# A gated linear-attention and Mish MLP kernel: the SBUF pool moved up by 128 bytes, and the queries' denominators kept in an existing tile

## The chip, the cores and the metric

The kernel runs on one core of a Trainium2 chip, in one launch. The metric is the device time of one execution in microseconds (us), given as the median of several runs. The profile is one further execution, recorded instruction by instruction.

Engines are named as in the profile: PE (TensorE matmuls), PEld (TensorE's weight loads), DVE (VectorE), ACT (ScalarE), POOL (GpSimd), SP (SyncE, which issues most DMAs). A matmul has a *moving* operand, which is streamed through the array (512 columns here), and *weights*, the stationary operand, which a separate weight load puts into the array beforehand. Both lie in SBUF.

## The reference

x is 2048 x 512. Attention has 32 heads of width 16; the MLP is 1376 wide.

```python
g = sigmoid((x * gate_w).sum(-1, keepdims=True))
return g * A(x) + (1 - g) * B(x)

# A: linear attention with a learned feature map
q, k, v = split_heads(x @ wqkv)
pq, pk  = q @ w_phi[h], k @ w_phi[h]                      # 16 x 16 for each head
phi_q   = concat([softmax(pq), softmax(-pq)], -1)         # 32 features
phi_k   = concat([softmax(pk), softmax(-pk)], -1)
kv, z   = sum_s(phi_k^T v), sum_s(phi_k)
o       = (phi_q @ kv) / (phi_q @ z + 1e-6)
A       = o @ wo

# B: MLP
B = mish(x @ w1 + b1) @ w2
```

## The kernel before

**Split precision.** Every large product is made of three matmuls in fp32r: an operand is split into a high part ("h") and a low part ("l"), and h\*h, h\*l and l\*h are added up in PSUM. So all tiles that feed 512-column matmuls come in pairs: `xh`/`xl`, `wvh`/`wvl`, `w1ah`/`w1al`, `w2ah`/`w2al`, and so on. The high part is written by ACT (a copy), the low part by DVE or POOL (a subtraction).

**Stages.** First (P0) the key and query weights are multiplied by the feature map (`fuse`). Then eight chunks A0 to A7 of 256 rows go through the projections (`proj`), the features of the keys (max, min, exp, sum on DVE and ACT, in tiles `E`), and the sums `kvp` and `z`. Chunks 2 to 7 use a Strassen-like scheme: sums of the weights and of the rows stand in spare parts of the MLP's weight buffers, so that `proj` matmuls there have operands named `w1bhr`, `w1blr`, `w2bh`, `w2bl`. Then four blocks B0 to B3 of 512 rows do, for the MLP, `up` (moving: `xbh`/`xbl`; weights: slices of `w1a`/`w1b`) and `down` (moving: `w2a`/`w2b`; weights: slices of `h`/`l`), and for attention the queries' features, `num` and `wo` (moving: `woh`/`wol`; weights: slices of `ohl`). `up` has 12 matmuls of 512 columns for each of 11 units and block, in turn four of `xbh` with high weights, four of `xbh` with low weights, four of `xbl` with high weights.

**Order.** The order of all steps is written out by hand in `ORDER`, and each instruction is pinned to it (`pin`), so each engine runs its instructions in the order of that text. An engine that waits for another holds up all that stands behind it in its own order.

**The queries' denominators.** For each 128 rows of a block, on DVE: `dsum` reduces the products `T` to a tile `D` of 64 columns (two halves of 32 heads, tag `Dn`, two buffers); `dm` multiplies it by the swapped sums `S`; `de` adds the two halves into a tile `den` of 32 columns of its own (one buffer); `rd` takes its reciprocal in place; `sc` multiplies the swapped `S` by it and writes the factors into `D`; `es` (DVE or POOL) scales `E` by `D`; `tr` transposes `E` on DVE and `st` stores it by DMA.

**Where the tiles lie.** SBUF addresses below are bytes within a partition, as the compiled program of the kernel before has them. Tiles are put one behind the other: some constants, the "arena" of 45056 bytes (`nc.alloc_sbuf_tensor("arena", ...)`, into which the four `w1` tiles are placed by hand, line 121 on), the pool `const` (`onr`, `cst`, `ident`, `mask`, `kvb`), and the pool `sp` with all other tiles, in the order in which their tags first occur. All slices that 512-column matmuls take start at multiples of 512 bytes within their tile, so that a tile's own address decides the remainder modulo 256.

| tiles | address | modulo 256 |
|---|---|---|
| `w1bh`, `w1bl`, `w1ah`, `w1al` (arena) | 16512, 26752, 36992, 49280 | 128 |
| `onr` | 61568 | 128 |
| `cst` (128 bytes) | 62080 | 128 |
| `ident`, `mask`, `kvb` | 62208, 62720, 63232 | 0 |
| `io` and `v`; `xbh`/`wkh`, `xbl`/`wkl` | 65280 on; 71424, 79616 | 0 |
| `wvh`/`woh`, `wvl`/`wol`; `wqh` and `wql` (later `eT`) | 87808, 96000; 104192, 112384 | 0 |
| `w2ah`, `w2al`, `w2bh`, `w2bl`, `wc` | 120576 to 165632 | 0 |
| `act`, `h`, `l`, `xh`, `xl` (8 buffers) | 167680 to 194560 | 0 |
| `E` (4 buffers) | 180096; 196864, 209152, 215808 | 128; 0, 0, 0 |
| `ohl`, `xraw`, `T`, `pq`, `zb`, `Dn` and the rest | to 229120 | 0, but 128 for `mn` |
| `den` (128 bytes, the last tile) | 229120 | 0 |

So in `down` and `wo` and in most of `proj`, both operands lie at 0 modulo 256. In `up` the moving operand lies at 0 and the weights at 128. In some pairs of `proj` matmuls of chunks 2 to 7, one operand lies in the arena, at 128, and the other at 0.

Of the kernel before, what the change touches and what calls it, by code (L numbers as in the profile page):

```python
# [9 lines left out]
F32 = mybir.dt.float32  # L10
# [5 lines left out]
P = 128  # L16
S = 2048
D = 512
H = 32
# [70 lines left out]
def tile_gated_mix(ctx: ExitStack, tc: tile.TileContext, xT, wv, wkT, wqT, bd, w1a, w1b, b1, w2a, w2b, wo, out):  # L90
    nc = tc.nc
    const = ctx.enter_context(tc.tile_pool(name="const", bufs=1))
# [5 lines left out]
    V, G_, A_, Sy = nc.vector, nc.gpsimd, nc.scalar, nc.sync  # L98
# [4 lines left out]
    def pin(x):  # L103
        r = tc.keep_in_program_order(x)
        if hold[0] and dve and r.ins.engine == G_.engine:
            hold[0] = False
            tc.add_manual_dep(r.ins, dve[0].ins.name, SYNC, reason="VectorE's step first")
        return r
# [5 lines left out]
    def on_(e):  # L114
        return vv if e is V else pin
# [14 lines left out]
    def T(shape, dt, tag, bufs, name):  # L130
        if tag in FIXED:
            return FIXED[tag][dt]
        nm[0] += 1
        if bufs > 1 and slots:
            tag, bufs = tag + slots.pop(0), 1
        return sp.tile(shape, dt, name=f"{name}_{nm[0]}", tag=tag, bufs=bufs)

    def k8(name, tag, dt=F32R):
        return T([P, 2048], dt, tag, 1, name)

    def k4(name, tag, dt=F32):
        return T([P, 1024], dt, tag, {"E": 4, "tx": 2, "oh": 2, "z": 1}[tag], name)

    def k2(name, tag, dt=F32):
        return T([P, 512], dt, tag, {"pq": 2, "io": 4, "hl": 8}[tag], name)
# [14 lines left out]
    def hv(ap):  # L160
        return ap.rearrange("p (h f) -> p h f", f=DH)
# [32 lines left out]
    pin(G_.memset(md, 1.0))  # L194
    pin(G_.affine_select(md, md, pattern=[[-DH, 8], [0, DH]], compare_op=ALU.is_ge, fill=0.0, base=0, channel_multiplier=1))
    pin(G_.affine_select(md, md, pattern=[[DH, 8], [0, DH]], compare_op=ALU.is_ge, fill=0.0, base=DH - 1, channel_multiplier=-1))
    cst = const.tile([P, 32], F32, name="cst")
    b1s, g_sb, og_sb = cst[:, :NF], cst[:, 12:20], cst[:, 20:28]
    pin(G_.dma_start(b1s, b1))
    ident = const.tile([P, P], F32, name="ident")  # L200
# [9 lines left out]
    def at(key, name, fn):  # L210
        steps.setdefault((key, name), []).append(fn)
# [81 lines left out]
    def feat_ops(key, t, src, d, negative=False):  # L293

        n = str(t)

        def red(name, op):
            d[name] = T([P, H], F32, name, 2, name)
            pin(V.tensor_reduce(d[name], hv(src()), axis=AX.X, op=op))  # L299

        def dd(a, e=V):
            if "E" not in d:
                d["E"] = k4("E", "E")
            E = hv(d["E"][:, a * 512 : (a + 1) * 512])
            note = on_(e) if key[0] == "B" else pin
            if (a == 0) != negative:
                note(e.tensor_sub(E, hv(src()), d["mx"][:, :, None].to_broadcast([P, H, DH])))  # L307
            else:
                note(e.tensor_sub(E, d["mn"][:, :, None].to_broadcast([P, H, DH]), hv(src())))

        def ss():
            d["S"] = T([P, 2 * H], F32, "Sm", 2, "Sm")
            pin(V.tensor_reduce(d["S"], hv(d["E"][:, :]), axis=AX.X, op=ALU.add))  # L313

        at(key, "mx" + n, lambda: red("mx", ALU.max))
        at(key, "mn" + n, lambda: red("mn", ALU.min))
        for a in range(2):
            if key[0] == "B":
                for x, e in ENG:
                    at(key, f"d{a}{n}{x}", lambda a=a, e=e: dd(a, e))  # L320
            else:
                at(key, f"d{a}{n}", lambda a=a: dd(a))
        at(key, "E" + n, lambda: act(d["E"], d["E"], AF.Exp))
        at(key, "S" + n, ss)
        if key[0] == "A":
            at(key, "rS" + n, lambda: pin(V.reciprocal(d["S"], d["S"])))

    def scale_by(d, eng, by="S"):
        on_(eng)(eng.tensor_mul(hv(d["E"][:, :]), hv(d["E"][:, :]), d[by][:, :, None].to_broadcast([P, 2 * H, DH])))  # L329
# [346 lines left out]
    def b_ops(b):  # L676
        key = ("B", b)
# [88 lines left out]
        for t in range(4):  # L766
            d = {}
            i = 4 * b + t

            def lq(d=d, i=i):  # L770
                d["p"] = k2("pq", "pq")
                pin(Sy.dma_start(d["p"], pqd[i * P : (i + 1) * P, :]))

            def tm(e, d=d):
                d["T"] = k4("T", "tx")
                on_(e)(e.tensor_mul(d["T"], d["E"], B["zb"]))  # L776

            def dsum(d=d):
                d["D"] = T([P, 2 * H], F32, "Dn", 2, "Dn")
                pin(V.tensor_reduce(d["D"], hv(d["T"][:, :]), axis=AX.X, op=ALU.add))  # L780

            def halves(t):
                return t[:, :].rearrange("p (a h) -> p a h", a=2)

            def dm(d=d):
                pin(V.tensor_mul(halves(d["D"]), halves(d["D"]), halves(d["S"])[:, ::-1, :]))

            def de(d=d):
                d["d"] = T([P, H], F32, "den", 1, "den")
                pin(V.tensor_add(d["d"], d["D"][:, :H], d["D"][:, H:]))  # L790

            def sc(d=d):
                pin(V.tensor_mul(halves(d["D"]), halves(d["S"])[:, ::-1, :], d["d"][:, None, :].to_broadcast([P, 2, H])))

            def st(d=d, i=i):
                eTd[i] = tc.dram_tile([P, 1024], F32, name=f"eTd{i}")
                pin(Sy.dma_start(eTd[i][:, :], d["E"]))

            def ld(t=t, i=i):
                h = t // 2  # L800
                if h not in eTs:
                    eTs[h] = k8("eT", ("tt", "eT")[h], F32)[:, :].rearrange("p (t q x) -> p t q x", t=2, q=4)
                src = eTd[i].rearrange("(q i) (k x) -> k i q x", q=4, k=4)
                for k in range(4):
                    o = 64 * (k % 2) + 32 * (k // 2)
                    pin(Sy.dma_start(eTs[h][o : o + 32, t % 2, :, :], src[k]))

            at(key, f"lq{t}", lq)
            feat_ops(key, t, lambda d=d: d["p"][:, :], d)
            for x, e in ENG:  # L810
                at(key, f"T{t}{x}", lambda tm=tm, e=e: tm(e))
                at(key, f"es{t}{x}", lambda d=d, e=e: scale_by(d, e, "D"))
            at(key, f"D{t}", dsum)
            at(key, f"m{t}", dm)
            at(key, f"de{t}", de)
            at(key, f"rd{t}", lambda d=d: pin(V.reciprocal(d["d"], d["d"])))
            at(key, f"sc{t}", sc)
            at(key, f"tr{t}", lambda d=d: pin(V.transpose(d["E"][:, :], d["E"][:, :])))  # L818
            at(key, f"st{t}", st)
            at(key, f"ld{t}", ld)  # L820
# [60 lines left out]
    for b in range(NB):  # L881
        b_ops(b)
# [98 lines left out]
```

## Time and profile before

| | |
|---|---|
| median of 3 runs | 449.42 us (449.0 to 449.97) |
| the profiled execution | 449.53 us, of which the span from first to last instruction is 447.8 us |
| PE, PEld, DVE, ACT, POOL busy | 98%, 79%, 73%, 51%, 42% of the span |
| chain that ended last | PE 83%, DVE 13%, DMA 1%, issue 1% |
| its largest lines | `proj` 26%, `up` 22%, `down` 21%, `wo` 10% |
| TensorE clock granted | 0.996 of full speed |

A row of the profile's groups reads: line, engine, operation, output<-inputs, shapes, xcount, busy time in us, mean ns of one, idle time of that engine just before. For a matmul the moving operand is named ahead of the weights. The ends of matmuls are modelled, and neighbouring matmuls overlap, so that the busy time of one (some 390 ns) is not what it costs; the distance between starts is. The chain of waits gives such distances: it lists pieces as start in us, length in us, engine, tile, line and xcount, each piece reaching up to the start of the next one.

### The profile page before, as it was taken

To read this page: it belongs to the slowest core of one execution; us is meant where nothing else is said; L and a number is where in the kernel's file an instruction comes from. 1 tells how busy PE (TensorE), PEld (TensorE's weight loads), DVE (VectorE), ACT (ScalarE), POOL (GpSimd) and SP (SyncE) were. 2 spreads that over 40 slices of the span, in tenths; PEclk is the share of its full clock that TensorE was granted. 3 is DMA by queue.
4 is the path that set the end of the run, shared out by engine and by line. 5 is a ranking of instruction groups with operands and counts; after the bars stand their busy time and mean duration, and the time that the engine had idled before them with its cause. 6 is when DMAs were issued, how large, how long until landed. Compare 5 with 4: busy or idle time off the path is not lost.

```text
span 447.8 us, 7210 instructions
## 1 busy us (share of the span) xinstructions
PE 439.2 (98%) x2832; PEld 352.9 (79%) x2832; DVE 326.5 (73%) x433; ACT 227.7 (51%) x312; POOL 187.7 (42%) x139
## 2 busy tenths in 40 slices
PE   6999999999999999999999999999999999999996
PEld 5878888888788888877788878788887887888774
DVE  1699989998899799999896789337576673856212
ACT  4727626456465594863457375375452464243411
POOL 2466545668676166772325427330223021043110
PEclk8999999999999999999999999999999999999999
DMA  7422191988561342645133425002514301045202
GB/s 275 173 94 95 70 254 55 241 207 197 163 217 48 121 141 71 224 152 165 50 116 117 143 71 183 29 25 98 179 55 157 126 0 72 0 178 191 78 1 94
DMA packets 29033, 55.14 MB, mean 123 GB/s; under 512 B 5252, under 2 KB 13444, under 8 KB 29000
## 3 DMA queue, kind: packets, MB, share of 16 engines
q1 hardware_dynamic: 26952, 48.26, 31.7%
q0 software_dynamic: 1904, 6.17, 6.9%
q8 instruction: 22, 0.36, 0.3%
q10 hardware_dynamic: 144, 0.26, 0.2%
q14 instruction: 11, 0.09, 0.1%
HBM read 32.26 MB, written 22.03 MB: 121 GB/s over the span
## 4 chain that ended last, share of the span: by engine, by line
PE 83%; DVE 13%; DMA 1%; issue 1%; SPq 0%; ACT 0%; DVEq 0%
PE proj L128 26%; PE up L128 22%; PE down L128 21%; PE wo L128 10%; PE kvp L128 2%; DVE E L329 2%; PE num L128 2%; DMA w1ahf<-in_wkT_dram 1%; DVE Sm L313 1%; DVE Dn L780 1%; DVE den L790 1%; PE fuse L128 1%; DVE E L818 1%; DVE T L776 1%; DVE mn L299 1%
## 5 line engine op out<-in xcount | busy, mean ns | idle before, releaser
L701 POOL TENSOR_TENSOR l<-act,h 128x512 fp32r<-128x512 f32 x27 | 36.7, 1360 | 98.8 <-ACT h L155 89.4
L155 ACT ACTIVATE act<-up,cst 128x512 f32<-128x512 f32 x44 | 30.0, 686 | 56.4 <-PE up L128 44.9
L155 ACT ACTIVATE E<-E 128x1024 f32<-128x1024 f32 x32 | 33.5, 1057 | 19.3 <-DVE E L307 10.1
L128 PE MATMUL wo<-woh,ohl 128*128 128x512 f32 x128 | 42.0, 392 | 0.1
L155 ACT ACT_TABLE_LOAD x31 | 39.8, 1283 | 1.5 <-PE up L128 1.0
L155 ACT ACTIVATE h<-act 128x512 fp32r<-128x512 f32 (+1 forms) x48 | 30.1, 629 | 20.5 <-PE down L128 9.6
L313 DVE TENSOR_REDUCE Sm<-E 128x64 f32<-128x1024 f32 x32 | 38.5, 1205 | 2.4 <-ACT E L155 2.4
L128 PE MATMUL down<-w2ah,h 128*128 128x512 f32 x96 | 37.7, 392 | 0.0
L128 PE MATMUL down<-w2al,h 128*128 128x512 f32 x96 | 37.4, 390 | 0.0
L128 PE MATMUL down<-w2bh,h 128*128 128x512 f32 x80 | 31.9, 399 | 0.0
L128 PE MATMUL down<-w2ah,l 128*128 128x512 f32 x80 | 31.3, 391 | 0.0
L128 PE MATMUL down<-w2bh,l 128*128 128x512 f32 x80 | 31.3, 391 | 0.0
L128 PE MATMUL down<-w2bl,h 128*128 128x512 f32 x80 | 31.2, 390 | 0.0
L701 DVE TENSOR_TENSOR l<-act,h 128x512 fp32r<-128x512 f32 x13 | 11.9, 912 | 25.3 <-PE down L128 10.2
L128 PEld LDWEIGHTS wo<-woh,ohl 128*128 128x128 f32 x128 | 24.0, 188 | 5.8 <-DVE ohl L842 0.4
L867 DVE SCALAR_TENSOR_TENSOR io<-down,cst,io 128x512 f32<-128x512 f32 x16 | 11.6, 738 | 22.5 <-PE down L128 12.7
L818 DVE STREAM_TRANSPOSE E<-E 128x1024 f32<-128x1024 f32 x16 | 19.9, 1243 | 9.5 <-POOL E L329 9.1
L128 PE MATMUL up<-xbh,w1ahr 128*128 128x512 f32 x96 | 26.5, 397 | 0.0
L128 PE MATMUL up<-xbh,w1alr 128*128 128x512 f32 x96 | 26.2, 395 | 0.0
L776 POOL TENSOR_TENSOR T<-E,zb 128x1024 f32<-128x1024 f32 x7 | 18.1, 2582 | 19.5 <-ACT E L155 19.5
L128 PE MATMUL up<-xbl,w1ahr 128*128 128x512 f32 x96 | 26.2, 394 | 0.0
L842 DVE TENSOR_TENSOR ohl<-num,ohl 128x512 fp32r<-128x512 f32 x16 | 10.5, 686 | 21.3 <-ACT ohl L155 21.2
(195 smaller groups left out, 1102.6 us busy)
## 6 DMA issues: line engine op xcount, KB each, us to landing
eTd<-E SPq DMA_DIRECT2D x16, 512.0 KB, 3.0
eT<-eTd SPq DMA_DIRECT2D x64, 128.0 KB, 3.0
xraw<-in_xT_dram SPq DMA_DIRECT2D x15, 512.0 KB, 4.6
zd<-E POOLq DMA_DIRECT2D x10, 512.0 KB, 7.3
pqd<-qs SPq DMA_DIRECT2D x16, 256.0 KB, 2.6
pq<-pqd SPq DMA_DIRECT2D x16, 256.0 KB, 2.8
out_dram<-io SPq DMA_DIRECT2D x16, 256.0 KB, 2.1
raw<-in_w2a_dram SPq DMA_DIRECT2D x3, 512.0 KB, 5.1
```

Source lines behind the costliest of these rows:

```text
L128: return pin(nc.tensor.matmul(*a, **k))
L155: return pin(A_.activation(out_, in_, fn, **k))
L299: pin(V.tensor_reduce(d[name], hv(src()), axis=AX.X, op=op))
L313: pin(V.tensor_reduce(d["S"], hv(d["E"][:, :]), axis=AX.X, op=ALU.add))
L329: on_(eng)(eng.tensor_mul(hv(d["E"][:, :]), hv(d["E"][:, :]), d[by][:, :, None].to_broadcast([P, 2 * H, DH])))
L701: on_(e)(e.tensor_sub(U[i]["l"], U[i]["a"], f32(U[i]["h"])))
L776: on_(e)(e.tensor_mul(d["T"], d["E"], B["zb"]))
L780: pin(V.tensor_reduce(d["D"], hv(d["T"][:, :]), axis=AX.X, op=ALU.add))
L790: pin(V.tensor_add(d["d"], d["D"][:, :H], d["D"][:, H:]))
L818: at(key, f"tr{t}", lambda d=d: pin(V.transpose(d["E"][:, :], d["E"][:, :])))
L842: pin(V.tensor_sub(ohl[h, gp][:, 512:], num[h, gp], f32(ohl[h, gp][:, :512])))
L867: pin(V.scalar_tensor_tensor(io[t], dn[t], og_sb[:, i % 8 : i % 8 + 1], io[t], op0=ALU.mult, op1=ALU.add))
```

## The change

The tile `cst` grows from 32 to 64 columns (128 to 256 bytes for each partition); its parts stay where they are, and the added columns are used by nothing. The tile `den` is gone: the sum of the halves is written over the first half of `D`, its reciprocal is taken there, and `sc` now reads `S` in its own order and writes the halves of `D` in swapped order, the second half first, so that the denominators are overwritten last.

```diff
-    cst = const.tile([P, 32], F32, name="cst")
+    cst = const.tile([P, 64], F32, name="cst")
     b1s, g_sb, og_sb = cst[:, :NF], cst[:, 12:20], cst[:, 20:28]
...
+            def den(d):
+                return d["D"][:, :H]
+
             def de(d=d):
-                d["d"] = T([P, H], F32, "den", 1, "den")
-                pin(V.tensor_add(d["d"], d["D"][:, :H], d["D"][:, H:]))
+                pin(V.tensor_add(den(d), den(d), d["D"][:, H:]))
 
             def sc(d=d):
-                pin(V.tensor_mul(halves(d["D"]), halves(d["S"])[:, ::-1, :], d["d"][:, None, :].to_broadcast([P, 2, H])))
+                pin(V.tensor_mul(halves(d["D"])[:, ::-1, :], halves(d["S"]), den(d)[:, None, :].to_broadcast([P, 2, H])))
...
-            at(key, f"rd{t}", lambda d=d: pin(V.reciprocal(d["d"], d["d"])))
+            at(key, f"rd{t}", lambda d=d: pin(V.reciprocal(den(d), den(d))))
```

No instruction is added or taken away, and `ORDER` stays as it is.

## The prediction

> **What bounds the kernel now.** First the page's own lines: the profiled execution took 449.53 us with a span of 447.8, so 1.7 us lie around the span; the sum below is made against 449.53, which is 0.11 above the median of the runs (449.42).
>
> ```profile
> span 447.8 us, 7210 instructions
> PE 439.2 (98%) x2832; PEld 352.9 (79%) x2832; DVE 326.5 (73%) x433; ACT 227.7 (51%) x312; POOL 187.7 (42%) x139
> ```
>
> PE is never long without work, but its busy time is made of modelled ends. So I read next the chain of waits, in which a piece of matmuls reaches up to the next piece: length by count is the distance between starts. From it, in order of time:
>
> ```profile
> 139.94 2.80 PE up L128 x12
> ...
> 146.84 2.80 PE up L128 x12
> 149.64 1.97 PE kvp L128 x128
> 151.63 0.04 DVE km L645
> ...
> 204.44 1.18 DVE wol L617
> 205.62 0.61 DVE ohl L842
> 206.23 0.04 issue
> 206.28 5.32 PE wo L128 x22
> ...
> 222.37 16.75 PE up L128 x72
> ```
>
> ```profile
> 327.98 12.27 PE down L128 x54
> ...
> 391.23 8.37 PE up L128 x36
> 399.60 6.81 PE down L128 x30
> ...
> 418.09 2.73 PE wo L128 x12
> ...
> 443.74 0.75 DVE io L867
> ```
>
> Two things are to be seen. From 30 us to 151.6 and from 206.28 to 443.7 the chain is PE alone; between 151.63 and 206.2 it is DVE, whose steps follow each other without a wait for PE, until `wo` needs `wol` and `ohl`. PE is full there too, but it ends that stretch waiting, 0.4 us by the list of PE's waits:
>
> ```profile
> PE wo L128 <- DVE wol L617: 0.4, 1, 0.4
> ```
>
> And the same 128x512 matmul does not cost the same everywhere. `up`: 16.75/72 = 232.6 ns and 8.37/36 = 232.5, from start to start. `down`: 12.27/54 = 227.2 and 6.81/30 = 227.0. `wo`: 2.73/12 = 227.5. All three are of one shape and type and run at one clock. What sets `up` apart in the table of addresses is that its moving operand starts at 0 modulo 256 bytes and its weights at 128; in `down` and `wo` both start at 0. The difference is 5.2 to 5.4 ns; I take 5.2, since a row of `down` just behind `up` is a little slower than 227.
>
> Chunks 2 to 7 say more, since there operands in the arena mix with others from one pair of matmuls to the next. The timeline of PE in chunk 3 (start, modelled length, moving operand ahead of the weights):
>
> ```profile
> 93.71 0.62 PE L128 MATMUL proj<-wkh,xh 128*128 128x512 f32 x2
> ...
> 95.07 0.62 PE L128 MATMUL proj<-w2bh 128*128 128x512 f32 x2
> 95.53 0.62 PE L128 MATMUL proj<-w1blr,w2bh 128*128 128x512 f32 x2
> 95.98 0.63 PE L128 MATMUL proj<-w2bh,w1bhr 128*128 128x512 f32 x2
> 96.45 0.62 PE L128 MATMUL proj<-w2bl,w2bh 128*128 128x512 f32 x2
> ...
> 97.83 1.07 PE L128 MATMUL proj<-wvh,xh 128*128 128x512 f32 x4
> ```
>
> Six matmuls with all operands at 0 (93.71 to 95.07) take 1.36 us, 226.7 ns each; the six from 95.07 to 96.45, with one pair of mixed operands either way, take 1.38, and so do the next six.
>
> **The change part by part.**
>
> *The layout.* `cst` grows by 128 bytes, so all that is allocated behind it lies 128 bytes higher: `xbh`, `w2a`, `w2b`, `h`, `l`, `ohl`, `woh` and the other tiles of the pool go from 0 to 128 modulo 256. The arena and `onr` lie ahead of `cst` and stay at 128. Both operands of every 512-column matmul are then at 128: no mixed pair is left, and no pair is at 0 and 0. The trace of before has no long run with both at 128, so its price is bounded. Lower end: the pair that is alike at 0, 227.2 ns (nothing in the rows excludes one a little faster, but none shows it). Upper end: 232.6 ns, the price of weights at 128, if it is the weights' own remainder that costs. I take the lower end, because of the chunk's rows. If weights at 128 cost 5 ns by themselves, that had to show where they are loaded beside a moving operand that is at 128 too, which happens once in each such term: the load for `w2bh,w1bhr` runs beside the last matmul of the pair `w1blr,w2bh`. That pair took 95.98 - 95.53 = 0.45 us, 225 ns each, no more than an all-0 pair; the pair after it, moving at 0 and weights at 128, took 0.47, 235 each. The evidence is thin (one load for each term), and it speaks for the relation of the two operands.
>
> How many matmuls are concerned comes from the groups, first and last of the six of `up` (three of 96, three of 80: 528) and of the six of `down` (two of 96, four of 80: 512), the two of `wo` and the first of three of 64 that read `wv`:
>
> ```profile
> L128 PE MATMUL up<-xbh,w1ahr 128*128 128x512 f32 x96 | 26.5, 397 | 0.0
> ...
> L128 PE MATMUL up<-xbh,w1blr 128*128 128x512 f32 x80 | 21.8, 395 | 0.0
> L128 PE MATMUL down<-w2ah,h 128*128 128x512 f32 x96 | 37.7, 392 | 0.0
> ...
> L128 PE MATMUL down<-w2bl,h 128*128 128x512 f32 x80 | 31.2, 390 | 0.0
> L128 PE MATMUL wo<-woh,ohl 128*128 128x512 f32 x128 | 42.0, 392 | 0.1
> ...
> L128 PE MATMUL wo<-wol,ohl 128*128 128x512 f32 x64 | 25.1, 391 | 0.4 <-DVE wol L617 0.4
> L128 PE MATMUL proj<-wvh,xh 128*128 128x512 f32 x64 | 17.3, 393 | 0.0
> ```
>
> - `up` in B1 to B3: three quarters of 528 are 396, all behind 206.28, where the chain is PE: 396 x 5.2 ns = 2.06 us.
> - `up` in B0 ahead of 151.63: the two pieces of 12 at 139.94 and 146.84: 24 x 5.2 = 0.12 us.
> - the other 108 of B0: 0.56 us of PE time, but between 151.63 and 206.2, where DVE's chain sets when `wol` and `ohl` are there. PE would come to that wait 0.56 us earlier and wait 0.56 us longer: nothing.
> - `proj` in chunks 2 to 7: five terms of six matmuls a chunk use arena operands, 30 terms at 1.38 - 1.36 = 0.02 us: 0.6 us, all ahead of 151.63, where the chain is PE.
>
> Together 2.8 us. What is late next: in B1 to B3 PE is 2 us quicker over 240 us, and the steps that feed it (`h`, `l`, `ohl` by ACT, DVE and POOL) must keep up. DVE is busy 65% there by the stage from 260 to 330 us:
>
> ```profile
> 260.00:330.00 70.00, 70.00 (x361) 55.83 (x360) 45.42 (x70) 39.09 (x50) 23.74 (x14) 1.00 0.31 102
> ```
>
> So there is slack on the whole, but the order is fixed and some step will sit tight. I take 0.1 us off for that; its bounds are nothing and all 2.06.
>
> *Other engines and the DMAs on moved tiles.* ACT's copies of the same shape and type write `w1ah` at 128 and `w2ah` at 0, and the loads of 256 KB fill `w1ah` at 128 and the first `xraw` at 0:
>
> ```profile
> L155 ACT ACTIVATE w2ah<-raw 128x1024 fp32r<-128x1024 f32 x3 | 3.2, 1055 | 2.4 <-DMA raw<-in_w2a_dram 2.4
> ...
> L155 ACT ACTIVATE w1ahr<-raw 128x1024 fp32r<-128x1024 f32 x3 | 3.1, 1044 | 0.0
> ```
>
> ```profile
> w1ahf<-in_wkT_dram SPq DMA_DIRECT2D x4, 256.0 KB, 6.0
> ...
> xraw<-in_xT_dram SPq DMA_DIRECT2D x2, 256.0 KB, 6.0
> ```
>
> 1044 against 1055 ns and 6.0 against 6.0 us: no price of the remainder, nothing taken.
>
> *The denominators.* The four steps keep their counts, and DVE runs them in its own order, so no wait is added and none goes:
>
> ```profile
> L790 DVE TENSOR_TENSOR den<-Dn 128x32 f32<-128x32 f32 x16 | 10.0, 623 | 0.4
> L816 DVE RECIPROCAL den<-den 128x32 f32<-128x32 f32 x16 | 5.6, 347 | 0.4
> ...
> L793 DVE TENSOR_TENSOR Dn<-Sm,den 128x64 f32<-128x64 f32 x16 | 4.8, 300 | 0.4
> ```
>
> They are the same shapes with another output address. Were each of the 48 slower or faster by 20 ns, a fifteenth of `sc`, only the 12 in B0's DVE stretch would count, 0.24 us either way. I take nothing. In B1 to B3 the cover is DVE's idle time; if it is gone, another 0.7 us at most.
>
> The sum: 449.53 - 2.06 - 0.12 - 0.6 + 0.1 = 446.85, which I round to 446.8 since the median stands 0.11 lower.
>
> **A rule that speaks against the change.** The Trainium skill, "SBUF — State Buffer", section "Who interferes with whom", gives PE two independent SBUF read ports, one for the moving operand and one for weight loads, and says that "PE and ACT never wait on anyone". By that, addresses that are multiples of 16 bytes, as all are here, should not matter to a stream of matmuls, and the change is worth nothing: 449.5. The trace disagrees at least in part, with 232.6 ns beside 227.2 for one shape.
>
> **The rivals.**
>
> *Weights at 128 cost by themselves.* Then it isn't the mixture: a start off the 256-byte boundary costs, and the change gives that price to every matmul instead of taking it from `up`. For it: every slow `up` matmul has weights at 128, and a mixed pair with the moving operand at 128 looks cheaper (0.45 us) than one with the weights there (0.47). Against it: the load beside the pair at 95.53. Place and price: `down` 512, `wo` 192, `wv` 192, the key and query projections 168 and 84 pool-only ones in chunks 2 to 7 are 1148 matmuls newly at 128; some 100 of them lie in the DVE stretch, where PE has 0.4 us to spare; 1050 x 5.2 = 5.5 us more: 455.0. It decides from less than 1 ns a matmul on, since nothing stands against it then; were the moving operand's start to cost as well, it is worse.
>
> *The low address bits have nothing to do with it.* All operands at 128 are also all in the arena, so `up` may be slower because its weights come from a distant part of SBUF, or for how its matmuls follow each other. Then the change does not do what it says: 449.5. For it: position and remainder cannot be told apart in the trace. Against it: pool tiles up to 150 KB apart (`ohl` and `woh`) run at 227.
>
> *The gain is waited away.* PE gets faster, but in B1 to B3 the operands of `down` and `wo` come no sooner, as between 151.63 and 206.2. Then only 0.7 us remain: 448.8. For it: that stretch itself. Against it: PE's list of waits names none behind 206.3, and DVE has 35% idle.
>
> **How the numbers follow.** About 0.2% (0.9 us) is what a measurement of this kernel can tell from no change. Forecast 0.62 (446.8; its own range 446.2 to 447.9: 0.6 lower if the runs of 12 behind `up` get quicker too, 1.1 higher if half of the 2.06 is waited away); the bits do nothing 0.17 (449.5); waited away 0.05 (448.8); weights' own price 0.16 (455.0, slower). Faster is 0.62, same is 0.17 + 0.05 = 0.22, slower 0.16. The range leaves out the slower case and little else: 446.2 to 450.2, its upper end at no change plus what the denominators' steps could add in B0 and B1 to B3.
>
> **What would show it.** Right: in the chain of waits `up` x12 takes 2.72 to 2.74 us instead of 2.80, and a term of chunk 3 takes 1.36; `down` and `wo` stay at 227; PE's wait for `wol` grows from 0.4 to about 0.9. Wrong: `down` and `wo` rise to 232 (own price), `up` stays at 232 (other cause), or PE's list of waits gets new rows behind 206 us (waited away). A new DVE row on `Dn` longer than 300 ns in the mean would show that the denominators' new addresses cost.

## The result, and the profile after

The changed kernel takes 445.95 us (445.4 to 446.3), beside 449.7 for the kernel before in the same session: the ratio is 0.9913, with a 95% interval of 0.9888 to 0.9937. The forecast of 446.8 had the direction and the cause; the gain is larger than it said, and 445.95 lies 0.25 us below the range.

The page of the changed kernel, its span, busy times and granted clock; below it the clock's line of the page of before.

```profile
span 444.2 us, 7210 instructions
PE 435.4 (98%) x2832; PEld 353.1 (79%) x2832; DVE 326.0 (73%) x433; ACT 227.7 (51%) x312; POOL 187.7 (42%) x139
PEclk8899999999999999999999999999999999999999
```

```profile
PEclk8999999999999999999999999999999999999999
```

The chain of waits after, at the places by which the stretches below are cut, with a long piece of `up` and of `down`:

```profile
10.34 4.14 PE proj L128 x9
...
60.47 1.93 PE kvp L128 x128
...
151.86 0.04 DVE km L645
...
203.88 1.18 DVE wol L617
...
221.78 16.32 PE up L128 x72
...
325.58 12.24 PE down L128 x54
...
440.06 0.75 DVE io L869
```

And two lines of the chain of before that were not shown:

```profile
10.22 2.92 PE proj L128 x9
...
59.25 1.92 PE kvp L128 x128
```

`up` costs 16.32/72 = 226.7 ns instead of 232.6, and is now level with `down` (226.7) and `wo`. Cut at the same instructions, the two profiled executions compare like this (us):

| stretch | before | after | difference | forecast |
|---|---|---|---|---|
| start to the first `kvp` | 59.25 | 60.47 | +1.22 | none |
| first `kvp` to `km` | 92.38 | 91.39 | -0.99 | -0.72 for all up to `km` |
| `km` to `wol` (DVE's chain) | 52.81 | 52.02 | -0.79 | 0 |
| `wol` to the last `io` | 239.30 | 236.18 | -3.12 | -2.06 + 0.1 |

The first row isn't the change's. The same nine `proj` matmuls at 10 us, whose operands all lie in the pool, take 2.92 us in one execution and 4.14 in the other. By their starts they come some 0.43 us apart up to a certain moment and 0.23 from then on: before, that moment is 11.6 us; after, all nine are slow. From 11 to 15 us the granted clock is 0.93 before and 0.56 after. Kernels with the layout of before start late as well: with matmuls added behind its end (below) the kernel before itself took 4.14 us there and came to `kvp` at 60.57; with the denominators alone it is 60.20, with the layout turned round 59.82. So the profile of before, against which the forecast was summed, began on the lucky side, and from the first `kvp` on the change brings 4.90 us.

### The profile page after: what moved, and what is told of

Its sections match the earlier page's. It is cut to its first block, busy times and chain, and to the rows that moved or that the text cites. A ratio compares the mean times of both kernels' runs of the same rounds, so it can differ in the third digit from the quotient of the medians.

```text
span 444.2 us, 7210 instructions
## 1 busy us (share of the span) xinstructions
PE 435.4 (98%) x2832; PEld 353.1 (79%) x2832; DVE 326.0 (73%) x433; ACT 227.7 (51%) x312; POOL 187.7 (42%) x139
## 4 chain that ended last, share of the span: by engine, by line
PE 83%; DVE 13%; DMA 1%; issue 1%; SPq 0%; ACT 0%; DVEq 0%
PE proj L128 27%; PE up L128 22%; PE down L128 21%; PE wo L128 10%; PE kvp L128 2%; DVE E L329 2%; PE num L128 2%; DMA w1ahf<-in_wkT_dram 1%; DVE Sm L313 1%; DVE Dn L780 1%; DVE Dn L792 1%; PE fuse L128 1%; DVE E L820 1%; DVE T L776 1%; DVE mn L299 1%
## 5 line engine op out<-in xcount | busy, mean ns | idle before, releaser
L701 DVE TENSOR_TENSOR l<-act,h 128x512 fp32r<-128x512 f32 x13 | 11.6, 894 | 23.9 <-PE down L128 10.2
L869 DVE SCALAR_TENSOR_TENSOR io<-down,cst,io 128x512 f32<-128x512 f32 x16 | 11.6, 739 | 22.0 <-PE down L128 12.3
```

Of the source, the lines that this page charges most:

```text
L701: on_(e)(e.tensor_sub(U[i]["l"], U[i]["a"], f32(U[i]["h"])))
L869: pin(V.scalar_tensor_tensor(io[t], dn[t], og_sb[:, i % 8 : i % 8 + 1], io[t], op0=ALU.mult, op1=ALU.add))
```

## The experiments

**The two halves of the change.** The wider `cst` alone:

```diff
-    cst = const.tile([P, 32], F32, name="cst")
+    cst = const.tile([P, 64], F32, name="cst")
...
-                d["d"] = T([P, H], F32, "den", 1, "den")
+                d["d"] = cst[:, 32:64]
```

> The wider cst alone: the pool lies 128 bytes higher as in the changed kernel, but the denominators keep a place of their own (columns 32 to 63 of cst) and their old instructions. Theory (the two operands' remainders must agree, the denominators are worth nothing): as the changed kernel, 445.9 us, up x12 in 2.72 us. Rival (the rewritten denominators bring the part of the gain that I had not forecast): 447 us, with DVE's stretch from km to ohl at 54.0 us as before instead of 53.2.

445.16 us beside 450.24, ratio 0.9886 (0.9868 to 0.9903). The denominators alone (the changed kernel with `cst` back at 32 columns):

```diff
-    cst = const.tile([P, 64], F32, name="cst")
+    cst = const.tile([P, 32], F32, name="cst")
```

> The rewritten denominators alone, with cst at its old 128 bytes, so that the pool stays at 0 modulo 256. Theory: no change from before, 449.6 us, up x12 in 2.80 us, DVE's stretch from km to ohl about 54.0 us. Rival (the denominators give part): 448.5 us, with that stretch about 53.2 us.

450.39 us beside 450.24, ratio 0.9997 (0.9987 to 1.0006). The chain of waits of the layout alone, then of the denominators alone:

```profile
151.85 0.04 DVE km L645
...
203.88 1.18 DVE wol L617
...
221.78 16.32 PE up L128 x72
```

```profile
152.58 0.04 DVE km L645
...
205.40 1.18 DVE wol L617
...
223.29 16.75 PE up L128 x72
```

The layout does all of it, and the shorter DVE stretch (52.03 us here, 52.82 with the denominators alone) comes with the layout too, although the denominators' steps lie in that stretch. The denominators only make the room.

**The mixture turned round.** The arena at 0, the pool at 128:

```diff
+    nc.alloc_sbuf_tensor("front", [P, 32], F32)
     nc.alloc_sbuf_tensor("arena", [P, sum(FIXED.values())], F32)
...
-    cst = const.tile([P, 64], F32, name="cst")
+    cst = const.tile([P, 32], F32, name="cst")
```

> 128 bytes put ahead of the arena and cst at its old size, with the rewritten denominators: now the arena lies at 0 modulo 256 and the pool at 128, the mixture of before turned round (up: moving at 128, weights at 0). Theory (agreement of the two decides, in either direction): slow as before, 449.6 us, up x12 in 2.80 us. Rival 1 (it costs only when the weights are at 128 and the moving operand at 0): up x12 in 2.72 us and about 446 us. Rival 2 (a moving operand at 128 beside weights at 0 costs about half, as the pairs of chunk 3 seemed to say): up x12 in 2.76 us, 448 us.

450.14 us, ratio 1.0002 (0.9993 to 1.0012). Its chain of waits:

```profile
222.92 16.75 PE up L129 x72
```

The weights' own remainder is ruled out: with weights at 0 and the moving operand at 128, `up` costs the same 232.6. Rival 2, half the price for this direction, falls too; the pairs of chunk 3 on which it rested were too short to show a price.

**All at another remainder.** 64 bytes ahead of the arena, `cst` at 64 columns, all operands at 192:

```diff
+    nc.alloc_sbuf_tensor("front", [P, 16], F32)
     nc.alloc_sbuf_tensor("arena", [P, sum(FIXED.values())], F32)
```

> 64 bytes ahead of the arena and the wider cst: all operands at 192 modulo 256. Theory (only agreement counts): as the changed kernel, 445.9 us, up, down and wo x12 all 2.72 us. Rival (multiples of 128 are needed): every 512-column matmul slower, 5 ns by 1776 is 9 us: up to 455 us.

445.69 us beside 450.24, ratio 0.9894 (0.9877 to 0.9911); `up` x72 takes 16.32 us and `down` x54 12.24, as in the changed kernel. Common remainders of 128 and 192 are equal, and a common 0, in `down` of before, reaches 6.81/30 = 227.0.

**How near is near enough.** The changed kernel with `cst` at 48 and 80 columns (several executions each), then at 40, 56 and 72 (one execution each). Every edit is this line with another count:

```diff
-    cst = const.tile([P, 64], F32, name="cst")
+    cst = const.tile([P, 48], F32, name="cst")
```

> The changed kernel with cst at 48 columns: the pool at 64 modulo 256, the arena at 128. Theory A (both operands must begin in the same half of a 256-byte line): 64 and 128 are in different halves, slow as before, 450.2 us, up x12 in 2.80 us. Rival B (the cost grows with the distance modulo 256, at most 128): half of it, up x12 in 2.76 us, about 448 us. Rival C (any difference costs all): as A here, and it differs from A in the pool at 192.

> The changed kernel with cst at 80 columns: the pool at 192 modulo 256, the arena at 128. Theory A (same half of a 256-byte line): fast as the changed kernel, up x12 in 2.72 us, 0.989 of before. Rival B (distance): 64 apart as in the run with the pool at 64, up x12 in 2.76 us. Rival C (any difference): up x12 in 2.80 us, as before.

> cst at 40 columns: pool at 32 modulo 256, arena at 128 (up: moving at 32, weights at 128). With the pool at 0 and 64 up x12 took 2.80 us, at 128 2.72, at 192 2.75. Theory (a stretch of positions from 128 to 256 is cheaper than the lower half): 2.80 us here. Rival (every other 32 bytes behaves otherwise): 2.72 to 2.76 us.

> cst at 56 columns: pool at 96 modulo 256, 32 bytes below the arena's 128. Theory (the halves of a 256-byte line decide first): 2.80 us for up x12. Rival (nearness decides): 2.74 us or less.

> cst at 72 columns: pool at 160 modulo 256, 32 bytes above the arena's 128. Theory (same half, and inside it a price that grows with the distance): between 2.72 and 2.75 us for up x12. Rival (any difference at all costs at least what 64 bytes cost): 2.75 us or more.

One row of each kernel's chain of waits, in the order 32, 64, 96, 160, 192:

```profile
223.36 16.86 PE up L128 x72
```

```profile
223.12 16.80 PE up L128 x72
```

```profile
223.53 16.79 PE up L128 x72
```

```profile
222.80 16.79 PE up L128 x72
```

```profile
223.21 16.48 PE up L128 x72
```

| pool, with the arena at 128 | 0 | 32 | 64 | 96 | 128 | 160 | 192 |
|---|---|---|---|---|---|---|---|
| `up`, ns a matmul | 232.6 | 234.2 | 233.3 | 233.2 | 226.7 | 233.2 | 228.9 |

With the pool at 64 the time is 450.41 us, ratio 1.0000 (0.9990 to 1.0011); at 192 it is 448.03, ratio 0.9945 (0.9930 to 0.9961). My first theory, of halves of a 256-byte line, missed at 192 already (2.75 us for 12 instead of 2.72), and it fell with 160: 32 bytes away in the same half cost the whole price. A price growing with the distance fell as well, since 96, the nearest from below, is dear. What holds is nearly the third rival: a difference costs all, but for one of seven places, 64 above, which costs a third (2.2 of 5.9 ns). Why that place is cheap isn't settled.

**What a mixed run leaves behind it.** Seven runs of 24 matmuls behind the end of the kernel before, with a new PSUM tile for each run:

```diff
     run(ORDER)
+    w1h, w1l = [FIXED[n][F32R] for n in ("w1ah", "w1al")]
+    h2, l2 = w2at
+    for mv, wt, other in ((h2, l2, None), (h2, w1h, None), (h2, l2, 1), (w1l, l2, None), (h2, l2, 1), (w1l, w1h, None), (h2, l2, 1)):
+        slots[:] = "0"
+        ps = psum("bench", "a")
+        for i in range(24):
+            m, w = (l2, h2) if other and i // 4 % 2 else (mv, wt)
+            mm(ps, w[:, 128 * (i % 4) : 128 * (i % 4) + 128], m[:, 512 * (i % 4) : 512 * (i % 4) + 512], start=(i == 0), stop=(i == 23))
```

> The kernel before with seven runs of 24 matmuls of 512 columns added behind its end (their results are used by nothing), in this order: both operands at 0 modulo 256 (w2ah, w2al); moving at 0 and weights at 128; both at 0; moving at 128 and weights at 0; both at 0; both at 128 (w1al, w1ah); both at 0. The third, fifth and seventh run change tiles every four matmuls, so that the trace shows how they begin. Theory (each mixed run also makes the agreeing matmuls behind it slow for a while, which the forecast left out): the agreeing runs of 24 take 5.44 us (226.7 ns each), the mixed ones 5.58 (232.5), and the first fours behind a mixed run 0.93 us instead of 0.907, some 20 to 30 ns a run in all. Rival (the extra gain in down and wo came from something else): every four behind a mixed run 0.907 from the start on.

The timeline of PE (start, modelled length): both mixed runs, the run with both at 128, and the fours behind them.

```profile
450.55 5.85 PE L128 MATMUL bench<-w2ah,w1ahr 128*128 128x512 f32 x24
456.46 1.20 PE L128 MATMUL bench<-w2ah,w2al 128*128 128x512 f32 x4
457.50 1.08 PE L128 MATMUL bench<-w2al,w2ah 128*128 128x512 f32 x4
...
462.26 5.86 PE L128 MATMUL bench<-w1alr,w2al 128*128 128x512 f32 x24
...
473.96 5.73 PE L128 MATMUL bench<-w1alr,w1ahr 128*128 128x512 f32 x24
479.75 1.20 PE L128 MATMUL bench<-w2ah,w2al 128*128 128x512 f32 x4
480.79 1.07 PE L128 MATMUL bench<-w2al,w2ah 128*128 128x512 f32 x4
```

Prices agree: two operands at 128 are 0.12 to 0.13 us cheaper over 24 than a mixture of either direction. For what it was built for, the run is inconclusive: a new tile makes PE wait, and the first four behind any run, mixed (1.04 us) or not (1.04), carry that wait. So it was repeated with one tile throughout:

```diff
     run(ORDER)
+    w1h = FIXED["w1ah"][F32R]
+    h2, l2 = w2at
+    seq = [0] * 48 + [1] * 48 + [0] * 48 + ([1] * 4 + [0] * 4) * 12 + [0] * 48
+    slots[:] = "0"
+    ps = psum("bench", "a")
+    for i, mixed in enumerate(seq):
+        w = w1h if mixed else l2
+        mm(ps, w[:, 128 * (i % 4) : 128 * (i % 4) + 128], h2[:, 512 * (i % 4) : 512 * (i % 4) + 512], start=(i == 0), stop=(i == len(seq) - 1))
```

> The kernel before with 288 matmuls of 512 columns added behind its end, all into one PSUM tile so that nothing waits between them (the sum is used by nothing); moving always w2ah (at 0), weights w2al (at 0, agreeing) or w1ah (at 128, mixed): 48 agreeing, 48 mixed, 48 agreeing, then twelve times 4 mixed and 4 agreeing, then 48 agreeing. Theory (a mixed stretch leaves the agreeing matmuls behind it slow for some nine matmuls, about 15 to 20 ns a turn in all): the long stretches 48 x 232.5 = 11.16 us and 48 x 226.7 = 10.88 + 0.02; the alternating 96, with the same counts as the two long stretches before them, take 0.2 us more or above, 22.25 us instead of 22.05. Rival (each matmul has its price and no memory of what ran before): 22.05 us, equal to the sum of the two long stretches.

```profile
443.77 11.05 PE L128 MATMUL bench<-w2ah,w2al 128*128 128x512 f32 x48
454.66 11.32 PE L128 MATMUL bench<-w2ah,w1ahr 128*128 128x512 f32 x48
465.82 11.05 PE L128 MATMUL bench<-w2ah,w2al 128*128 128x512 f32 x48
476.71 1.10 PE L128 MATMUL bench<-w2ah,w1ahr 128*128 128x512 f32 x4
477.64 1.08 PE L128 MATMUL bench<-w2ah,w2al 128*128 128x512 f32 x4
478.56 1.10 PE L128 MATMUL bench<-w2ah,w1ahr 128*128 128x512 f32 x4
...
498.03 11.95 PE L128 MATMUL bench<-w2ah,w2al 128*128 128x512 f32 x52
```

Long runs: 454.66 - 443.77 = 10.89 us, 226.9 ns each, and 465.82 - 454.66 = 11.16, 232.5 each. From 476.71 to 498.03 there are 48 mixed and 44 agreeing matmuls (the last four stand in the row of 52): 21.32 us. At the long runs' prices they would take 11.16 + 44 x 0.2269 = 21.14. So 0.18 us over 11 full turns and a half, 16 ns a turn: in size about what was expected (0.2 for twelve), and not the rival's nothing.

But the theory's reason for it is not borne out. The 48 agreeing matmuls behind the 48 mixed ones take 476.71 - 465.82 = 10.89 us, as long as the 48 ahead of them: by their starts the first takes 232 ns and the second 227, so no nine are slow. In the alternating part, too, the cost lies elsewhere: the first of each mixed four takes 241 ns (in the long mixed run every seventh takes about that), and of each agreeing four the first, and the last ahead of a mixed one, take 231 and 232, the two between them 226 to 228.

**`up` alone.** Two tiles of 128 bytes are moved, so that `xbh` and `xbl` alone agree with the arena:

```diff
+    sp.tile([P, H], F32, name="lead", tag="mx0", bufs=1)
+    wkh, wkl = [kt(k8(n, t), 512) for n, t in (("wkh", "xbh"), ("wkl", "xbl"))]
+    sp.tile([P, H], F32, name="trail", tag="mn0", bufs=1)
-    wkh, wkl, wvh, wvl, wqh, wql = [
+    wvh, wvl, wqh, wql = [
```

> The kernel before with the two tiles mx and mn of 128 bytes moved around xbh and xbl, so that xbh and xbl alone lie at 128 and agree with the arena; everything else of the pool is at 0. up agrees then in all blocks; the mixed pairs of chunks 2 to 7 stay, and the key projections (moving in xbh and xbl's place) become mixed. Theory (what the forecast missed behind 151.6 us are matmuls that a mixed run slows after it, and DVE steps in B0 that wait for PE by way of POOL): from km on all is as in the changed kernel, DVE's stretch from km to wol 52.0 us instead of 52.8 and from there to the end 236.2 us instead of 239.3, while the time up to km is 0.5 to 1 us longer than before: about 446.5 us. Rival (DVE's stretch got shorter by the other tiles' places): 52.8 us there, and about 447.5.

446.83 us beside 450.2, ratio 0.9914 (0.9897 to 0.9930).

```profile
59.52 1.92 PE kvp L128 x128
...
152.24 0.04 DVE km L648
204.43 1.18 DVE wol L620
...
222.33 16.33 PE up L128 x72
...
441.17 0.75 DVE io L870
```

From the first `kvp` to `km` 92.72 us, 0.34 longer than before and not the 0.5 to 1 expected; DVE's stretch 52.19, which is 0.6 of the 0.8 us, so that most of it follows `up` and not the other tiles' places; from `wol` to the end 236.74. The last is 0.56 more than in the changed kernel and 0.4 more than expected from an all-agreeing stage. No 512-column `up`, `down` or `wo` is mixed there, but `up` has both at 128 and `down` both at 0. That the turns between the two cost this was not tried by itself.

## Why the prediction was right and wrong

**Right.** The mechanism: that a matmul's two operands must agree modulo 256 bytes to be fast, and that the trace of before showed it as `up` against `down` and `wo`. A remainder modulo 512 is not needed: after the change `xbh` (71424 + 128) and `w1ah` (36992) lie 135 times 256 bytes apart, and `up` is fast. A term of chunk 3 takes 1.36 us now (95.88 to 97.24), as forecast:

```profile
95.88 0.62 PE L128 MATMUL proj<-w2bh 128*128 128x512 f32 x2
...
97.24 0.62 PE L128 MATMUL proj<-w2bl,w2bh 128*128 128x512 f32 x2
```

That the denominators are worth nothing and that nothing is waited away behind 206 us also held. The load on which I rested the choice between the two ends for the price at 128 and 128 decided the right way, on thin evidence as the forecast said: such short pairs misled on the price of one direction. The rival of the weights' own price is ruled out by the run that turns the mixture round and the one that moves all to 192, the rival by which the low address bits do nothing by the layout alone. The rule weighed in the prediction (the Trainium skill, "SBUF — State Buffer", "Who interferes with whom": PE's two read ports are independent, PE never waits on anyone) would have made the change worth nothing; the runs here disagree with what I drew from it, by 5.9 ns a matmul. Whether the two reads meet in SBUF, or where else the time goes, no run here shows.

**Wrong: three terms of the sum.**

*`up` at 5.2 ns, and `down` and `wo` at nothing.* "I take 5.2, since a row of `down` just behind `up` is a little slower than 227" turned evidence for a further gain into a deduction. Behind 206 us the 24 pieces of `up` sum to 92.59 us before and 90.21 after: 2.38 us or 6.0 ns a matmul, not 2.06. And the 37 pieces of `down` sum to 94.01 before and 93.34 after, 0.67 us that had no term at all (`wo` gained another 0.1). One of these pieces in the chain of before, then after:

```profile
245.60 3.66 PE down L128 x16
```

```profile
244.44 3.63 PE down L128 x16
```

By the starts of all matmuls in the trace of before, the nine agreeing ones behind a mixed one are slow in the mean (233 ns for the first, 228 to 230 up to the seventh), and from the tenth on it is about 227. Behind 206 us that comes to 0.64 us at 24 places, 27 ns each, which is nearly all of the 0.67; in the trace of after it is nothing. With `up` alone made to agree it is 0.15 us. So the mixture is the cause. Why the slowness lasts so long here stays open, since behind the 48 mixed matmuls of the added run it lasted for one.

*DVE's stretch at nothing.* "between 151.63 and 206.2, where DVE's chain sets when `wol` and `ohl` are there" was said to be deaf to PE, since the chain showed no wait for it. It became 0.79 us shorter. PE's wait for `wol`, which the forecast had growing to about 0.9 us, stayed at 0.4. POOL, DVE and ACT in the timeline of before, then of after (idle time ahead and its cause in brackets):

```profile
169.06 1.30 POOL L701 TENSOR_TENSOR l<-act,h 128x512 fp32r<-128x512 f32 x1 [2.45 <-ACT h L155]
170.31 1.06 POOL L307 TENSOR_TENSOR E<-pq,mx 128x512 f32<-128x512 f32 x1
...
195.81 1.29 POOL L701 TENSOR_TENSOR l<-act,h 128x512 fp32r<-128x512 f32 x1 [1.17 <-ACT h L155]
```

```profile
170.45 1.00 DVE L786 TENSOR_TENSOR Dn<-Dn,Sm 128x64 f32<-128x64 f32 x1
...
196.32 0.86 DVE L786 TENSOR_TENSOR Dn<-Dn,Sm 128x64 f32<-128x64 f32 x1
```

```profile
195.10 0.63 ACT L155 ACTIVATE h<-act 128x512 fp32r<-128x512 f32 x1 [2.08 <-PE down L128]
```

After:

```profile
170.16 1.07 POOL L307 TENSOR_TENSOR E<-pq,mx 128x512 f32<-128x512 f32 x1
...
195.24 1.29 POOL L701 TENSOR_TENSOR l<-act,h 128x512 fp32r<-128x512 f32 x1 [0.75 <-ACT h L155]
```

```profile
170.74 0.56 DVE L786 TENSOR_TENSOR Dn<-Dn,Sm 128x64 f32<-128x64 f32 x1
...
196.16 0.45 DVE L786 TENSOR_TENSOR Dn<-Dn,Sm 128x64 f32<-128x64 f32 x1
```

```profile
194.53 0.63 ACT L155 ACTIVATE h<-act 128x512 fp32r<-128x512 f32 x1 [1.66 <-PE down L128]
```

The multiply `dm`, 64 columns wide, ends 0.07 to 0.08 us after POOL's instruction in all four places (171.45 after 171.37, 197.18 after 197.10; 171.30 after 171.23, 196.61 after 196.53), however early it starts, and each `dm` that begins while POOL is idle takes 0.21 to 0.23 us: it is held until POOL is done. The Trainium skill ("SBUF — State Buffer", "Who interferes with whom") says that a DVE instruction with two SBUF inputs contends with a GpSimd instruction that reads SBUF; these rows agree.

POOL's `l` starts when ACT has written `h`. At the second place the profile names PE's `down` as what ACT's `h` waited for, and in all four `h` begins 0.02 or 0.03 us behind the start of a `down` matmul (168.35 after 168.32 and 195.10 after 195.08; 168.20 after 168.18 and 194.53 after 194.51). `down` stands behind `up` in PE's order. So PE does reach DVE's chain, by way of ACT, POOL and a blocked instruction, which the chain books as DVE's own busy time.

Counted from `km`, the first `dm` ends at 19.82 us before and 19.44 after, 0.38 earlier; the second begins 0.39 and ends 0.80 earlier; and `wol` comes 0.79 earlier. So in these two executions the two steps account for the whole of it. The stretch followed `up` in the other kernels too: 52.8 us with `up` at 232.6 (before, and with the denominators alone), 52.35 at 228.9 (pool at 192), 52.0 at 226.7, and 52.19 where `up` alone agrees.

*The chunks at 0.02 us a term.* 0.72 us was forecast up to `km`, 0.99 came from the first `kvp` on: the price was read off two rows with 10 ns steps, and the turns there were not counted. By single starts, 0.41 us of it is the mixed `proj` matmuls, another 0.41 the agreeing ones, and 0.15 `up`.

The sum had 2.7 us, from the first `kvp` on 4.90 came; the profile's late start of 1.22 us took part of it away again in the one execution, so that the error looks smaller there. That the median came within 0.25 us of the range is luck of this kind: the layout alone, timed beside 450.24 us, brought 5.08. The range was too narrow at its lower end for the same reason: it allowed 0.6 us for the runs behind `up` and nothing for DVE's stretch.

## What to carry to other kernels

Look up where both operands of the large matmuls start, modulo 256 bytes, before counting on one price per shape: equal remainders gave 226.7 ns here and unequal ones up to 234, and 128 unused bytes ahead of a pool repaired it. Compare rows of the same shape across tiles by the distance between starts, and count the turns between kinds as well as the matmuls; a row that is a little slower than its kind, behind another kind, was a cost that could be removed here, and not noise. A chain that shows no wait for an engine may still hang on it: where a small instruction takes several times its usual time, see what ran on the neighbouring engine and what that one had waited for.

## What the runs showed of the hardware that I had not expected

- At 128 bytes apart the price of unequal starts is symmetric: 16.75 us for 72 matmuls with weights at 128 and moving at 0, and 16.75 with the two exchanged.
- It has no slope: 32 bytes apart, above or below, cost as much as 128 (233.2 against 232.6 ns) and 96 below cost 234.2, while 64 above cost 228.9 and 64 below 233.3.
- Turns cost as well, but not one sum each: alternating fours of mixed and agreeing matmuls took 16 ns a turn more than long runs of the same, one turn behind 48 mixed ones left no more than 0.01 us, and in the kernel `down` behind `up` lost 27 ns a place, over some nine matmuls.
- A small DVE multiply that began beside a POOL instruction ended just after it, 0.07 to 0.08 us in the four places above, and so took up to 1.00 us instead of 0.21 to 0.23.
